# A second feed-forward block whose inner layer is multiplied as seven products of sums, with the inner features taken in two halves

## The chip, the core and the metric

The kernel runs on one core of one Trainium2 chip. The metric is the device time of that core in microseconds (us): 1461.32 us is the median of three runs (1461.11 to 1463.19). The engines of the core are called PE (TensorE, matrix products), DVE (VectorE), ACT (ScalarE), POOL (GpSimd) and SP (SyncE, which here issues most of the DMA transfers). PE writes its sums into PSUM, which has eight banks; a bank holds one result of 128 rows by up to 512 numbers in fp32.

## The reference, cut to what matters

Three stages follow one another: an attention with head mixing (batch 4, 12 heads, 448 positions), a gated feed-forward layer, and a second feed-forward layer. Attention gives 1792 tokens of 768 features. The feed-forward weights arrive as 64-bit floats.

```python
# x: 1792 x 768, from attention
gate = 1.0 / (1.0 + np.exp(-(x @ w_gate)))        # 768 -> 1536
x = (gate * (x @ w_val)) @ w_out                  # 1536 -> 768
h = x @ w2_in                                     # 768 -> 2048
out = (h * (1.0 / (1.0 + np.exp(-1.702 * h)))) @ w2_out   # 2048 -> 768
```

## The kernel before, in words

Attention comes first; its order is worked out by a planner and the change leaves it as it is. Then the class `Ffn` works through the 1792 tokens in two blocks of 896 (two batches of 448, called h = 0 and 1). Each block passes four stages, named after the PSUM tile in which PE sums: gate and value (`pg`, `pv`; in the second block `pq`), `py` (w_out), `ph` (w2_in) and `po` (w2_out).

Numbers are kept as two parts: a rounded high part (a copy or cast on ACT) and the rest (a subtraction on DVE, here called the low part). A product of two such numbers takes three matmuls: high by high, high by low, low by high. A weight piece is 128 x 384, that is three 128 x 128 tiles; one step of the pipeline takes one piece, its "unit". In the first block each piece is loaded as 64-bit floats, converted by one ACT pass and four DVE passes (`bits`, `conv1` to `conv4`), stored in DRAM (`kept`) and split into high and low (`high`, `low`, L732 and L737). In the second block the pieces come back from `kept`, two per load, and are only split. `take` and `ahead` issue these steps some units before PE needs them; five buffers of split weights (pool `w`) limit how far. What is put off with `after(n, f)` is issued n+1 units later, behind that unit's weight work.

In the second block, gate and value are already done as seven products of sums in place of eight (`quarters`): the activations are cut into four quarters (two token halves by two halves of the 768 features), the weights of two neighbouring feature tiles too, and seven combinations are multiplied, 14 units of 9 matmuls for a gate-and-value pair of tiles (`ORDER`: 1, 2, 6, 5, 7, 4, 3, each for q = 0 gate and q = 1 value). DVE forms the weight sums (`sum`, L707) and, in `finish` (L845), the sums of the products, ACT saves three running sums per q (`save`, L841). The activation sums for it are formed during `po` of the first block (`next_x`).

`ph` is made of 16 feature tiles, each two units of 18 matmuls (128 x 448), all eight quarter products. `gated` (L809 to L815) then takes, for one token half after the other, the sigmoid (ACT), the product with the sum in PSUM (DVE) and the two parts. `po` sums all 16 feature tiles in PSUM for two column halves n of 384: 16 units of 21 matmuls (seven token tiles by three), for which it holds four pairs of banks. At the end of each n the seven sums are copied out by DVE and ACT in turn (L1003) and stored (L1005).

PSUM is handed out in pairs of banks by `banks` (L802). Every engine works through its own instructions in the order in which they were issued, so the order of the code is the order of the work.

Of the kernel before, what the change touches and what calls it, by code (L numbers as in the profile page):

```python
# [518 lines left out]
class Ffn:  # L519
# [9 lines left out]

    KG = 3  # L530
# [7 lines left out]
    def __init__(self, ctx, tc, xd, kept, w_gate, w_val, w_out, w2_in, w2_out, out):  # L538
# [18 lines left out]
        for n in range(self.NN):  # L557
            self.pieces += [self.block(w2_out, k0, 1, n * self.PW, self.PW) for k0 in range(K2)]
        self.N0 = len(self.pieces)

        self.items = [(i, i + 1) for i in range(self.N0)]
        self.units = [None] * self.N0
        for j in range(0, K1, 2):
            at = len(self.units)
            n = len(self.items)
            for f in range(2):
                for g in range(2):
                    self.items.append((4 * (j + f) + 2 * g, at + (10 + g if f == 0 else 14 + g)))
            for p in self.ORDER:
                for g in range(2):  # L570
                    self.units.append((p, n + g, n + 2 + g))
        for i in range(o1, self.N0, 2):
            at = len(self.units)
            self.units += [(0, len(self.items), x) for x in range(2)]
            self.items.append((i, at + 3))
# [14 lines left out]
    def open(self):  # L590
# [4 lines left out]
        self.xy_p = pool("xy", 2 * self.KD + 1, **rt)  # L595
# [3 lines left out]
        p0 = pool("ps0", 2, space=PSUM, **rt)  # L599
        self.pools = [p0, p0]  # L600
        self.X = [[self.form() for _ in range(2)] for _ in range(self.KD)]

    def form(self):

        return self.xy_p.tile([128, 2, self.S], F32R, tag="xy", name="xy")
# [39 lines left out]
    def early(self, i):  # L645
        if len(self.going) <= i:
            acc = self.banks(("pg", "pv")[i])
# [11 lines left out]
    def stage(self):  # L659
        i = self.items[len(self.staged)][0]  # L660
        st = self.wst_p.tile([128, self.PW, 2], U32, tag="ws", name="ws")
        if len(self.staged) < self.N0:
# [7 lines left out]
    def bits(self, i):  # L670
        if i < self.N0:
            c = self.wc_p.tile([128, self.PW], U32, tag="wc", name="wc")
            self.nc.scalar.activation(c.bitcast(F32), self.staged[i][:, :, 1].bitcast(F32), AF.Abs)
            self.conv[i] = c

    def conv1(self, i):
        if i < self.N0:
# [4 lines left out]
    def conv2(self, i):  # L682
        if i < self.N0:
# [4 lines left out]
    def conv3(self, i):  # L688
        if i < self.N0:
            c = self.conv[i]  # L690
            self.nc.vector.scalar_tensor_tensor(out=c, in0=self.staged[i][:, :, 1], scalar=0xC0000000, in1=c,  # L691
                                                op0=ALU.bitwise_and, op1=ALU.bitwise_or)

    def conv4(self, i):
        if i < self.N0:
            c = self.conv[i]
            self.nc.vector.scalar_tensor_tensor(out=c, in0=self.staged[i][:, :, 0], scalar=29, in1=c,  # L697
                                                op0=ALU.logical_shift_right, op1=ALU.bitwise_or)
            self.nc.sync.dma_start(self.kept[i], c.bitcast(F32))

    def sum(self, i):

        if self.units[i] is None or self.units[i][0] == 0:
            return
        p, n0, n1 = self.units[i]
# [358 lines left out]
```

## Time and profile before

| what | value |
|---|---|
| median of three runs | 1461.32 us |
| the profiled execution's own time | 1458.4 us |
| its span in the trace | 1456.7 us |
| PE busy | 1425.2 us, 98% of the span, 9264 matmuls |
| DVE busy | 919.2 us, 63%, 2180 instructions |
| ACT busy | 732.2 us, 50%, 1694 instructions |
| `pq`, second block (974.2 to 1127.5 us) | PE never idle, DVE busy 114.67 of 153.3 us |

The table is read from the top: the span says how long the core worked, the busy times how much of it each engine had an instruction under way. Busy times count an instruction from its start to its acknowledged end, so two neighbouring ones overlap a little; how often an engine can start one is read from the starts in a list by time. Matmuls overlap in the same way: one lasts some 365 ns in the record and the next begins about 203 ns after it.

### The profile page before, as it was taken

How to read it: one execution, taken by the hardware profiler on the slowest of the kernel's cores; microseconds unless marked ns; L12 is line 12 of the kernel's file. 1: busy time of each engine (PE TensorE's matmuls, PEld its weight loads, DVE VectorE, ACT ScalarE, POOL GpSimd, SP SyncE). 2: the span in 40 equal slices, each digit the busy share in tenths (PEclk: the TensorE clock that was granted, in tenths of full speed). 3: DMA queues.
4: the chain of work that ended last, by engine and by line, in shares of the span. 5: the costliest groups of instructions: out<-in, count | busy, mean ns of one | idle time of the engine just before them, and what ended most of it. 6: DMA issues, size and time to landing. Idle time of an engine off the chain costs nothing.

```text
span 1456.7 us, 25413 instructions
## 1 busy us (share of the span) xinstructions
PE 1425.2 (98%) x9264; PEld 1304.6 (90%) x9264; DVE 919.2 (63%) x2180; ACT 732.2 (50%) x1694; POOL 189.3 (13%) x175
## 2 busy tenths in 40 slices
PE   7999999999998999999999989999999999999998
PEld 5878888888887999999999889999999999999998
DVE  6677787787777767676667887757877223444121
ACT  6877887887886444433245443335555112443110
POOL 3343443443444000000000000000000000000000
PEclk9999999999999999999999999999999999999999
DMA  6645435422444645465635466722222211111121
GB/s 172 176 136 152 138 125 150 141 109 97 139 157 145 209 147 177 148 177 166 188 114 156 151 228 192 269 76 67 64 66 76 66 52 47 54 55 56 54 71 38
DMA packets 180045, 182.26 MB, mean 125 GB/s; under 512 B 66364, under 2 KB 175824, under 8 KB 179920
## 3 DMA queue, kind: packets, MB, share of 16 engines
q1 hardware_dynamic: 178896, 180.40, 40.1%
q8 instruction: 73, 1.20, 0.3%
q14 instruction: 52, 0.43, 0.1%
q10 hardware_dynamic: 960, 0.23, 0.1%
q0 software_dynamic: 64, 0.01, 0.0%
HBM read 104.31 MB, written 37.75 MB: 98 GB/s over the span
## 4 chain that ended last, share of the span: by engine, by line
PE 79%; DVE 9%; ACT 6%; DMA 4%; issue 2%; SPq 0%; POOL 0%; DVEq 0%; ACTq 0%; POOLq 0%
PE po L998 16%; PE py L793 12%; PE pq L836 11%; PE ph L793 9%; PE pso L325 7%; PE pv L793 6%; PE pg L793 6%; PE psv L344 5%; PE psp L280 4%; PE psq L240 3%; DMA ws<-in_moe_w_in_dram 2%; ACT ex L294 1%; DMA gt<-sc 1%; DVE wc L691 1%; DVE st L287 1%
## 5 line engine op out<-in xcount | busy, mean ns | idle before, releaser
L998 PE MATMUL po<-w,hx 128*128 128x384 f32 x1344 | 239.9, 340 | 3.4 <-DVE sg L814 2.6
L998 PEld LDWEIGHTS po<-w,hx 128*128 128x128 f32 x1344 | 238.8, 189 | 4.3 <-DVE sg L814 2.9
L793 PE MATMUL ph<-xy,w 128*128 128x448 f32 x1152 | 236.1, 366 | 1.9 <-DVE w L737 1.9
L793 PEld LDWEIGHTS ph<-xy,w 128*128 128x128 f32 x1152 | 215.7, 188 | 22.0 <-DVE w L737 4.9
L273 POOL TENSOR_TENSOR ghl<-gt,ghl 120x448 fp32r<-120x448 f32 (+1 forms) x151 | 174.0, 1158 | 259.6 <-ACT ghl L209 184.5
L325 PEld LDWEIGHTS pso<-w,ex 120*112 120x112 f32 (+1 forms) x1440 | 159.6, 177 | 29.9 <-ACT w L307 10.2
L325 PE MATMUL pso<-w,ex 120*112 120x120 f32 (+1 forms) x1440 | 171.7, 270 | 11.4 <-DVE xo L363 3.8
L793 PE MATMUL py<-g,w 128*128 128x448 f32 x864 | 176.0, 366 | 0.0
L793 PEld LDWEIGHTS py<-g,w 128*128 128x128 f32 x864 | 162.3, 188 | 13.4
L732 ACT CAST w<-wc 128x384 fp32r<-128x384 f32 x136 | 69.8, 513 | 160.7 <-DVE wc L697 115.0
L737 DVE TENSOR_TENSOR w<-ws,w 128x384 fp32r<-128x384 f32 x124 | 68.6, 554 | 127.2 <-ACT w L732 127.2
L732 ACT CAST w<-ws 128x384 fp32r<-128x384 f32 x124 | 62.1, 513 | 170.3 <-PE po L998 85.4
L280 PE MATMUL psp<-ghl,wphl 120*120 120x448 f32 x540 | 137.5, 383 | 2.4 <-POOL ghl L273 1.5
L287 DVE TENSOR_REDUCE st<-psp 120x1 f32<-120x448 f32 x180 | 108.5, 614 | 41.2 <-PE psp L280 40.8
L294 ACT ACTIVATE ex<-psp,st 120x448 f32<-120x448 f32 x180 | 113.0, 631 | 11.7 <-DVE st L287 7.2
L280 PEld LDWEIGHTS psp<-ghl,wphl 120*120 120x120 f32 x540 | 89.1, 182 | 16.3 <-issue 3.9
L209 ACT CAST ghl<-gt 120x448 fp32r<-120x448 f32 (+1 forms) x139 | 77.8, 563 | 50.6 <-PE psp L280 44.2
L814 DVE TENSOR_TENSOR sg<-sg,ph 128x448 f32<-128x448 f32 x64 | 39.8, 622 | 96.3 <-ACT sg L813 96.3
L836 PE MATMUL pq<-xy,w 128*128 128x448 f32 x468 | 98.0, 365 | 0.0
L836 PEld LDWEIGHTS pq<-xy,w 128*128 128x128 f32 x468 | 87.9, 188 | 7.1
L793 PE MATMUL pg<-xy,w 128*128 128x448 f32 x432 | 91.2, 368 | 0.0
L793 PE MATMUL pv<-xy,w 128*128 128x448 f32 x432 | 89.5, 365 | 0.0
(86 smaller groups left out, 1950.2 us busy)
## 6 DMA issues: line engine op xcount, KB each, us to landing
gt<-sc SPq DMA_DIRECT2D x172, 210.0 KB
kept<-wc SPq DMA_DIRECT2D x136, 192.0 KB
ws<-kept SPq DMA_DIRECT2D x68, 384.0 KB
ws<-in_moe_w_out_dram SPq DMA_DIRECT2D x56, 384.0 KB
ws<-in_moe_w_in_dram SPq DMA_DIRECT2D x32, 384.0 KB
ws<-in_moe_w_gate_dram SPq DMA_DIRECT2D x24, 384.0 KB
ws<-in_moe_w_val_dram SPq DMA_DIRECT2D x24, 384.0 KB
nat<-in_k_dram SPq DMA_DIRECT2D x48, 112.0 KB
```

Of the source, the lines that this page charges most:

```text
L209: (eng.copy if eng is nc.scalar else eng.tensor_copy)(dst, src)
L273: eng.tensor_tensor(out=t[:m, 1], in0=gt.pop(s)[:m], in1=t[:m, 0].bitcast(F32), op=ALU.subtract)
L280: nc.tensor.matmul(ps[:m, :S], wphl[:m, wp, :m], t[:m, gp], start=(i == 0), stop=(i == 2))
L287: nc.vector.tensor_reduce(out=st[:m, 0:1], in_=pre[s][:m, :S], axis=AX.X, op=ALU.max, negate=True)
L294: nc.scalar.activation(t[:m], pre.pop(s)[:m, :S], AF.Exp, bias=st[:m, 0:1], scale=1.0, accum_out=st[:m, 1:2])
L325: nc.tensor.matmul(ps[:JC, c, :, :n], e[:m, c * JC:(c + 1) * JC], w[:m, :, :n], start=True, stop=True)
L344: nc.tensor.matmul(ps[a * 64:a * 64 + 64, r, :n], vt[b][:, g, c, :], a_t[:, c, g, :n], start=(c == 0), stop=(c == NJ - 1), tile_position=( ...
L732: self.nc.scalar.copy(w[:, 0], self.source(i))
L737: self.nc.vector.tensor_tensor(out=w[:, 1], in0=self.source(i), in1=w[:, 0].bitcast(F32), op=ALU.subtract)
L793: self.nc.tensor.matmul(acc[:, hb, :self.S], st, act[k0 + kc][hb][:, ap], start=(k0 + kc == 0 and part == 0 and ap == 0), stop=(k0 + kc == ...
L836: nc.tensor.matmul(x, st, A[p][c][:, ap], start=(first and c + part + ap == 0), stop=(c == self.KG - 1 and part == 1), skip_group_check=no ...
L998: nc.tensor.matmul(po[tk][:, :PW], HX[kc][:, part, tk * 128:(tk + 1) * 128], w[:, wp], start=(kc == 0 and part == 0 and wp == 0), stop=(kc ...
```

## The change

`ph` of the second block uses `quarters` too. `quarters` now takes a function `done` that says what becomes of a finished sum: `gates` is the old use, `inner` the new one (four feature tiles at a time; the sigmoid goes back into a PSUM bank and DVE multiplies by it from there). The activation sums are formed by `next_y` during `py` of the second block. The 2048 inner features are taken in two halves, in both blocks: eight tiles of `ph`, then `po` over these eight for both n, whose sums are kept in SBUF (`kept` tiles in pool `gh`); then the other eight, and `po` again, to which the kept sums are added. `banks` hands out single banks, `po` takes seven. `gated` issues both sigmoids, then both products, then both splits. `next_x` forms all of the second block's first activation sums in 12 units of the second `po` half. Pool `gh` has 12 buffers in place of 16; the 21 tiles of the sums have a pool of their own.

```diff
+    def inner(self, HX):
+        def done(q, f, h, y, bank):
+            self.after(0, lambda: self.nc.scalar.activation(bank, y, AF.Sigmoid, scale=1.702))
+            self.after(1, lambda: self.tt(y, y, bank, ALU.mult))
+            self.after(2, lambda: self.hilo(HX[2 * q + f][:, :, h * self.S:(h + 1) * self.S], y))
+        self.quarters(self.A, done)
...
     def gated(self, g, pg, pv, scale=1.0):
-        for h in range(2):
-            sg = self.temp("sg")
-            self.nc.scalar.activation(sg, pg[:, h, :self.S], AF.Sigmoid, scale=scale)
-            self.nc.vector.tensor_tensor(out=sg, in0=sg, in1=pv[:, h, :self.S], op=ALU.mult)
-            self.hilo(g[:, :, h], sg)
+        sg = [self.temp("sg") for _ in range(2)]
+        for h in range(2):
+            self.nc.scalar.activation(sg[h], pg[h][:, :self.S], AF.Sigmoid, scale=scale)
+        for h in range(2):
+            self.nc.vector.tensor_tensor(out=sg[h], in0=sg[h], in1=pv[h][:, :self.S], op=ALU.mult)
+        for h in range(2):
+            self.hilo(g[:, :, h], sg[h])
...
+    def next_y(self, m, py):
+        A, KG, S = self.A, self.KG, self.S
+        c = m % KG
+        x, y = (py[h][:, :S] for h in range(2))
+        if m < KG:
+            for p in (1, 7):
+                A[p].append(self.form())
+            t = self.ys[c] = [self.temp("ys") for _ in range(2)]
+            self.nc.scalar.copy(t[0], x)
+            self.nc.scalar.copy(t[1], y)
+            self.tt(x, t[0], t[1], ALU.subtract)
+            self.hilo(A[1][c], t[0])
+            self.hilo(A[7][c], x)
+        else:
+            for p in (2, 6, 5, 4, 3):
+                A[p].append(self.form())
+            t0, t1 = self.ys[c]
+            self.hilo(A[2][c], x)
+            self.tt(t1, t1, y, ALU.add)
+            self.tt(t0, t1, t0, ALU.subtract)
+            self.flush()
+            self.hilo(A[6][c], t0)
+            self.tt(x, x, t0, ALU.subtract)
+            self.hilo(A[5][c], t1)
+            self.hilo(A[4][c], y)
+            self.hilo(A[3][c], x)
...
-            for f in range(K2):
-                ph = self.banks("ph")
-                self.products(ph, Y)
...
+            for half in range(2):
+                HX = []
+                for f in range(0, HK, 4):
+                    for _ in range(4):
+                        HX.append(gh_p.tile([128, 2, 2 * S], F32R, tag="gh", name="hx"))
+                        if not t:
+                            ph = self.banks("ph", 2)
+                            self.products(ph, Y)
+                            self.gated(HX[-1].rearrange("p a (h s) -> p a h s", h=2), ph, ph, 1.702)
+                    if t:
+                        self.inner(HX[f:])
+                self.flush()
...
+                for n in range(self.NN):
+                    po = self.banks("po", NT)
+                    for kc in range(HK):
...
+                    self.flush()
                     for tk in range(NT):
+                        i = n * NT + tk
+                        if half == 0:
...
+                            (nc.scalar.copy if tk % 2 else nc.vector.tensor_copy)(kept[i], po[tk][:, :PW])
+                        else:
...
+                            if tk % 2:
+                                nc.scalar.copy(ot, po[tk][:, :PW])
+                                self.after(0, lambda ot=ot, i=i, out=out: (self.tt(ot, ot, kept[i], ALU.add),
+                                                                           nc.sync.dma_start(out, ot)))
+                            else:
+                                self.tt(ot, kept[i], po[tk][:, :PW], ALU.add)
+                                nc.sync.dma_start(out, ot)
+                    self.flush()
```

Three places show how the instructions move. The first is DVE in `ph` of the second block. Before, one feature tile (36 matmuls) is two low parts of weights (`w`), two products with the sum (`sg<-sg,ph`) and two low parts of results (`hx`):

```order
L819 TENSOR_TENSOR hx<-sg,hx 128x448 x2
L737 TENSOR_TENSOR w<-ws,w 128x384
L814 TENSOR_TENSOR sg<-sg,ph 128x448 x2
L737 TENSOR_TENSOR w<-ws,w 128x384
L819 TENSOR_TENSOR hx<-sg,hx 128x448 x2
```

Now a piece of the last six units of a group of four tiles, in the same stage (`wt` are sums of weights; `s<-s,pq` at L892 is `finish`, at L937 the product with the sigmoid):

```order
L892 TENSOR_TENSOR s<-s,pq 128x448
L937 TENSOR_TENSOR w<-ws,w 128x384
L743 TENSOR_TENSOR wt<-ws 128x384
L743 TENSOR_TENSOR wt<-ws,wt 128x384
L937 TENSOR_TENSOR c<-c,pq 128x448
L892 TENSOR_TENSOR s<-s,pq 128x448
L937 TENSOR_TENSOR w<-ws,w 128x384
L743 TENSOR_TENSOR wt<-ws 128x384
L743 TENSOR_TENSOR wt<-ws,wt 128x384
L937 TENSOR_TENSOR s<-s,pq 128x448
L864 TENSOR_TENSOR hx<-c,hx 128x448
L892 TENSOR_TENSOR s<-s,pq 128x448
```

What was 24 DVE instructions for four tiles is now 46, for 126 matmuls in place of 144.

The second place is ACT in `ph` of the first block, one feature tile with the two weight pieces behind it (`wc` and `w` are the passes on weights). Before:

```order
L813 ACTIVATE sg<-ph 128x448
L818 CAST hx<-sg 128x448
L813 ACTIVATE sg<-ph 128x448
L818 CAST hx<-sg 128x448
L673 ACTIVATE wc<-ws 128x384
L732 CAST w<-wc 128x384
```

Now:

```order
L768 CAST w<-wc 128x384
L856 ACTIVATE sg<-ph 128x448 x2
L863 CAST hx<-sg 128x448 x2
L709 ACTIVATE wc<-ws 128x384
L768 CAST w<-wc 128x384
```

The second sigmoid stands ahead of the first cast, which has to wait for DVE's product.

The third place is the end of the program on DVE, from the last parts of `ph` on. Before:

```order
L737 TENSOR_TENSOR w<-ws,w 128x384
L819 TENSOR_TENSOR hx<-sg,hx 128x448 x2
L737 TENSOR_TENSOR w<-ws,w 128x384 x15
L1003 COPY ot<-po 128x384 x4
L737 TENSOR_TENSOR w<-ws,w 128x384 x13
L1003 COPY ot<-po 128x384 x4
```

Now:

```order
L864 TENSOR_TENSOR hx<-s,hx 128x448 x3
L937 TENSOR_TENSOR w<-ws,w 128x384 x7
L937 TENSOR_TENSOR ot<-kept,po 128x384 x4
L937 TENSOR_TENSOR ot<-ot,kept 128x384 x3
L937 TENSOR_TENSOR w<-ws,w 128x384 x6
L937 TENSOR_TENSOR ot<-kept,po 128x384 x4
L937 TENSOR_TENSOR ot<-ot,kept 128x384 x3
```

The three additions for the sums that ACT copies stand behind DVE's own four.

## Rows read from the trace of the kernel before

**Rows 1.** The page: busy time of each engine, share of the span, instructions.
```profile
PE 1425.2 (98%) x9264; PEld 1304.6 (90%) x9264; DVE 919.2 (63%) x2180; ACT 732.2 (50%) x1694; POOL 189.3 (13%) x175
```

**Rows 2.** PE by time: start, length, line, tiles, count, idle time before and releaser.
```profile
642.64 86.58 PE L793 MATMUL py<-g,w 128*128 128x448 f32 x432
729.06 66.97 PE L793 MATMUL ph<-xy,w 128*128 128x448 f32 x328
796.29 7.56 PE L793 MATMUL ph<-xy,w 128*128 128x448 f32 x36 [0.26 <-DVE w L737]
...
850.00 0.34 PE L998 MATMUL po<-w,hx 128*128 128x384 f32 x1
851.12 3.27 PE L998 MATMUL po<-w,hx 128*128 128x384 f32 x17 [0.78 <-DVE w L737]
857.01 117.34 PE L998 MATMUL po<-w,hx 128*128 128x384 f32 x654 [2.62 <-DVE sg L814]
974.19 11.11 PE L836 MATMUL pq<-xy,w 128*128 128x448 f32 x54
...
996.30 14.76 PE L836 MATMUL pq<-xy,w 128*128 128x448 f32 x72
...
1021.81 14.76 PE L836 MATMUL pq<-xy,w 128*128 128x448 f32 x72
...
1127.52 89.44 PE L793 MATMUL py<-g,w 128*128 128x448 f32 x432
1216.80 116.91 PE L793 MATMUL ph<-xy,w 128*128 128x448 f32 x576
1333.55 118.95 PE L998 MATMUL po<-w,hx 128*128 128x384 f32 x672
```

**Rows 3.** Stretches: length, busy time of PE, PEld, DVE, ACT, POOL, PEclk, DMA.
```profile
857.00:861.00 4.00, 3.99 (x14) 3.99 (x15) 4.00 (x11) 2.01 (x4) 0.00 (x0) 0.57 0.36 98
...
974.20:1127.50 153.30, 153.30 (x757) 141.98 (x757) 114.67 (x223) 83.11 (x168) 0.00 (x0) 1.00 0.23 71
```

**Rows 4.** DVE by time in `ph` of the first block.
```profile
828.55 0.35 DVE L679 TENSOR_SCALAR wc<-wc 128x384 f32<-128x384 f32 x1
...
830.02 0.56 DVE L737 TENSOR_TENSOR w<-wc,w 128x384 fp32r<-128x384 f32 x1
831.13 0.62 DVE L814 TENSOR_TENSOR sg<-sg,ph 128x448 f32<-128x448 f32 x1 [0.56 <-ACT sg L813]
832.83 0.62 DVE L814 TENSOR_TENSOR sg<-sg,ph 128x448 f32<-128x448 f32 x1 [1.08 <-ACT sg L813]
```

**Rows 5.** DVE by time in `pq` of the second block.
```profile
994.35 0.62 DVE L851 TENSOR_TENSOR c<-c 128x448 f32<-128x448 f32 x1
994.88 0.61 DVE L845 TENSOR_TENSOR s<-s,pq 128x448 f32<-128x448 f32 x1
995.41 0.55 DVE L737 TENSOR_TENSOR w<-ws,w 128x384 fp32r<-128x384 f32 x1
995.88 0.55 DVE L707 TENSOR_TENSOR wt<-ws 128x384 f32<-128x384 f32 x1
```

**Rows 6.** ACT by line in `pq` (974.2 to 1127.5): busy, mean ns, idle before.
```profile
L732 ACT CAST w<-wt 128x384 fp32r<-128x384 f32 x48 | 24.6, 513 | 14.7 <-PE pq L836 9.3 <-ACT w L732 5.5
L841 ACT COPY s<-pq 128x448 f32<-128x448 f32 x36 | 19.2, 535 | 20.7 <-PE pq L836 19.7 <-ACT w L732 0.9
...
L848 ACT ACTIVATE s<-s 128x448 f32<-128x448 f32 x18 | 10.4, 578 | 0.6
L818 ACT CAST g<-s 128x448 fp32r<-128x448 f32 x17 | 9.7, 568 | 8.3 <-DVE s L851 8.3
```

**Rows 7.** The end by time, PE, DVE and SP's queue.
```profile
1445.81 6.70 PE L998 MATMUL po<-w,hx 128*128 128x384 f32 x37
...
1450.48 3.46 SPq L1005 DMA_DIRECT2D out_dram<-ot  x7
...
1452.01 1.09 DVE L1003 COPY ot<-po 128x384 f32<-128x384 f32 x2 [0.51 <-PE po L998]
```

More of the change, by code (lines that the diff above doesn't have):

```diff
@@ L556, in __init__, with whole, kept_pair, kept_sums @@
             self.pieces += [self.block(w2_in, k0, KG, f * 128, 128) for k0 in range(0, KD, KG)]
[L557 to L564, printed above, removed]
+        o2 = len(self.pieces) - 2 * K2
+        o3 = len(self.pieces)
+        HK = K2 // 2
+        for half in range(2):
+            for n in range(self.NN):
+                self.pieces += [self.block(w2_out, k0, 1, n * self.PW, self.PW) for k0 in range(half * HK, half * HK + HK)]
+        self.items = []
+        self.units = []
+        def whole(i):
+            self.units.append(("f", len(self.items), i))
+            self.items.append(("f", i, len(self.units)))
+        def kept_pair(i):
+            u = len(self.units)
+            self.units += [("p", len(self.items), x) for x in range(2)]
+            self.items.append(("k", i, u + 3))
+        def kept_sums(i):
+            u = len(self.units)
             n = len(self.items)
@@ L758, in ahead, with flush @@
     def ahead(self):
-        while self.step < min(self.taken + (4 if self.taken < self.N0 else 5), len(self.units) + 2):
+        n = 5 if self.units[self.taken - 1][0] == "s" else 4
+        while self.step < min(self.taken + n, len(self.units) + 2):
             self.split()
-        now, self.later = [f for n, f in self.later if n <= 0], [(n - 1, f) for n, f in self.later if n > 0]
-        for f in now:
-            f()
+        self.flush(False)
+    def flush(self, whole=True):
+        while self.later:
+            now, self.later = [f for n, f in self.later if n <= 0], [(n - 1, f) for n, f in self.later if n > 0]
+            for f in now:
+                f()
+            if not whole:
+                break
     def after(self, n, f):
@@ L800, in products, with banks @@
             pass
-    def banks(self, name):
-        self.turn += 1
-        return self.pools[(self.turn - 1) % len(self.pools)].tile([128, 2, 512], F32, tag="ps", name=name)
+    def banks(self, name, n):
+        self.turn += n
+        return [self.pools[i % len(self.pools)].tile([128, 512], F32, tag="ps", name=name)
+                for i in range(self.turn - n, self.turn)]
     def temp(self, name):
@@ L989, in run @@
[L989 to L1005 removed]
+                if t:
+                    self.next_y(m, py)
+                else:
+                    Y.append([self.form() for _ in range(2)])
+                    for h in range(2):
+                        self.hilo(Y[m][h], py[h][:, :S])
```

306 lines of the change are left out of this document (150 added, 156 removed).

## The prediction

> **What bounds the kernel now.** I read the page's engine line first, then PE by time over the second half, then the stretches by stage, then DVE and ACT inside the stages that change. PE is busy 1425.2 of 1456.7 us [rows 1]: what counts is how many matmuls there are and where PE waits. In PE by time the reader is to see two things. The second block's `ph` runs without a gap, 1333.55 - 1216.80 = 116.75 us for 576 matmuls, 202.7 ns each [rows 2]. The first block's `ph` does the same 576 from 729.06 to 850.00, 120.94 us: after nine of sixteen tiles (328 matmuls) PE begins to wait at each tile for DVE's low part of the weights, 0.26 us in the row shown. Then at the start of `po` it waits 0.78 and 2.62 us [rows 2]. Behind these waits the clock falls: granted 0.57 from 857 to 861, and full again later [rows 3]. `pq`, which works as the new stage will, has PE busy in all of its 153.3 us, DVE in 75% of it [rows 3].
>
> **The change part by part.**
>
> *Matmuls.* `ph` of the second block is 576 matmuls; seven of eight products make it 4 groups of 14 units of 9, that is 504. `po` keeps its 1344. So 72 go. A group of 126 took 1021.81 - 996.30 = 25.51 us in `pq` [rows 2], 202.5 ns each, the same as in `ph`. 72 x 0.2027 = **14.6 us saved**, if PE is fed as well as in `pq`.
>
> *Can DVE feed it?* DVE starts: from 994.35 to 994.88 and on to 995.41 an instruction of 448 columns takes 0.53 us, whether it reads SBUF alone or PSUM; one of 384 takes 0.47 [rows 5]. A group of `inner` has 46: 8 sums of `finish`, 8 products with the sigmoid and 8 low parts of results (24 x 0.53 = 12.7), 14 low parts and 8 sums of weights (22 x 0.47 = 10.3), together 23.1 us against 25.5 us of PE. `pq` has 38 (four products and four low parts of results fewer): 18.8. It is not even over the group. I stepped the issued order against unit ends 1.82 us apart: after units 8 to 13, which each end in a sum, DVE is up to some 2.5 us late; before, and in the three units that follow, it catches up. The low part of a weight stands in the order behind the sum of unit i and is needed by unit i+4, three units or 5.5 us later. So the lateness does not reach PE, with some 3 us to spare. ACT has 14 casts, 6 saves, 8 sigmoids and 8 casts of results: 14 x 0.513 + 6 x 0.535 + 8 x 0.578 + 8 x 0.568 = 19.6 us at most [rows 6], covered. The sigmoid that writes into PSUM has no row; by the nearest rows it lies between the save's 535 and the sigmoid's 578 ns [rows 6], 0.4 us per group on an engine with 6 us left, so nothing either way. I take zero for all this; if the cover is gone, each us that a group of DVE takes beyond 25.5 us is 4 us in all, less the 5.5 us of lead at the start of each half.
>
> The rows just read show no difference between an SBUF and a PSUM operand on DVE. The Trainium skill says otherwise: Perfetto Trace Analysis, Optimizing Scalar/DVE Operations, gives DVE about 60 ns of access overhead on SBUF and about 125 on PSUM. By that, the 16 instructions per group that read PSUM would cost 16 x 0.065 = 1.0 us more (an estimate from that page), 24.1 of 25.5 us; the sum would stay as it is, but rival B would be likelier, about one in five. By the rows it is one in eight, and I hold to the rows.
>
> *Waits of the first block.* In `ph` DVE works in a cycle of 7.84 us: ACT alternates sigmoid, cast, sigmoid, cast, and DVE waits 0.56 and then 1.08 us for the two sigmoids [rows 4]. Its own work is two weight pieces (four passes from 828.55 to 830.02 and 0.47 for the low part, 1.94 each) and four instructions of 0.53, 6.0 us; PE's tile is 36 x 0.2027 = 7.3 us. With both sigmoids ahead of the casts the 1.08 goes, and DVE is faster than PE. Besides, after eight tiles comes `po` for 16 units of 3.72 us, with 1.94 us of weights each: time to get ahead, and before, the first eight tiles had no wait. So the 120.94 - 116.75 = 4.2 us go. `po` of the first block took 974.19 - 850.00 = 124.19, of the second 1452.5 - 1333.55 = 118.95 [rows 2]; the 5.2 us between them are the two waits and the fallen clock. `po` took all eight banks and waited for the last pair's products; now it takes seven single ones, and the two banks of the last tile come to it as the seventh and not at all. I count **9.4 us saved**, from 0 (the waits turn up elsewhere) to 9.4.
>
> What takes their place? The new ends of `po` copy out seven sums while PE is at the last unit, bank by bank, and an eighth bank is free for the next: as at the middle of `po` today, where no wait is listed. Tightest is the second half of the first block, where 33 DVE instructions of `next_x` (17.5 us) now fall into 12 units instead of 32: steps 2 to 11 hold 20 x 0.97 + 17.5 + 3.3 for seven additions, 40.2 us, against ten units of 37.2. By the lookahead of `ahead` DVE is some two units (7 us) ahead there, so the 3 us are eaten from the lead. I take 0, with 0 to 3 us.
>
> *Sums in two steps.* 14 copies in each block: DVE 8 x 0.47, ACT 6, behind PE's last unit of a `po`; and additions in place of copies. Hidden, except at the end of the program: there DVE's three additions for ACT's sums stand behind its own four. Before, the last copy ended at 1453.1 and SP issued until 1453.94 [rows 7]; three times 0.47 put the last issue **1.4 us later**. Bounds 0 (the issues were the slower: seven in 3.46 us) and 2.5 (three transfers behind one another).
>
> *`next_y`.* During `py` of the second block, three or eight DVE instructions per 14.9 us step; nothing. After the last step the first units need their weights: three DVE instructions and one low part (2.1 us) stand ahead of the low part for unit 2, needed 3.7 us after the end of `py`. Close, covered.
>
> *Other placement.* Tiles get other addresses. That a stage's pace can differ is seen in `py`: the same 432 matmuls from 642.64 to 729.06 and from 1127.52 to 1216.80 [rows 2], 86.4 and 89.3 us, with no wait listed. I give the new 102 us of `inner` 3% of it either way, 3 us, and expect none.
>
> The sum against the profiled execution: 1458.4 - 14.6 - 9.4 + 1.4 = 1435.8 us. The median of the runs is 2.9 us above that execution, so **1438.7, say 1439 us**; its own range is 1434 to 1444.
>
> **The rivals.**
>
> *B, DVE bounds the new stage.* For: 23.1 of 25.5 us leaves little, and the first block's `ph` shows how waits for ACT make DVE the bound at less work, 1.64 us idle per two results [rows 4]. Against: there the sigmoid was issued just before the product that needs it, here two units ahead, and `pq` shows no wait. If each of the eight results of a group idled DVE by 0.82 us, a group takes 29.7 us, 4.2 us more, 16.7 in all: 1456. With half of that, 1447.
>
> *C, the first block's waits stay or move.* Then only 14.6 - 1.4 are won: 1448. For: DVE has 53% of its time in weights there, and there are now two starts of `po`. Against: the two sigmoids in a row, and the rest after eight tiles.
>
> *D, slower: the ring of seven temporaries.* A group of `inner` takes eight buffers of pool `s` (six saves, two `c`). The second save of a group gets the buffer that the sixth result of the group before gives back, which by my stepping DVE reads last some 3.4 us after ACT could begin. ACT works in order, so casts of weights behind it wait too. If DVE is later than I think, PE stops once in each of four groups: with 5 us each, and 4 us at the 0.57 of [rows 3] behind it (1.7 us lost), 27 us: 1466. It decides against the change from 5.6 us per group on, that is when DVE is 11 us late at the end of a group (5.5 of lead and 5.6). Against: I find 2.5.
> For that fall of the clock the Trainium skill has a rule too: TensorE: Matmul & The Clock Gate, A second HAM failure mode, tells of kernels whose groups cycle through PSUM banks and lose the clock in small gaps. The trace does not bear it out here: `pq`, in groups of 9 and with a bank for each sum, ran at 1.00 throughout [rows 3].
>
> That the change does not do what it says is excluded for the count: the order has 126 matmuls a group.
>
> **How the numbers follow.** The forecast has 0.70, B 0.12, C 0.08, D 0.07; 0.03 is for a loss of all that is won, about no change. The range goes from 1434 to 1452, which leaves out D, the upper half of B and the last: about 0.15. A measurement of this kernel tells a change from none at about 0.2%, 3 us. Faster: forecast, B and C, 0.90; same 0.03; slower 0.07.
>
> **What would show it.** Right: `ph` of the first block in two pieces of 58.4 us without a listed wait; `inner` in four groups of 25.5 us with PE busy throughout at clock 1.00 and DVE near 100% busy by the record; every `po` at 177 ns a matmul; the end 1.4 us longer. Wrong: PE in `inner` waiting for `w` from DVE (B) or ACT waiting for a low part of `hx` ahead of a save and PE behind it (D); a wait at the start of a `po` or in the last units of the first block (C); or the pace of a stage off by several per cent without a wait.

## The result and the profile after

The changed kernel ran in 1448.38 us (median of four runs, 1440.88 to 1452.13) against 1462.26 us before (four runs): a ratio of 0.9896, 95% interval 0.9848 to 0.9943. Timed twice more, later, it took 1446.7 us (ratio 0.9878, 0.984 to 0.9916) and 1442.03 us (0.9855, 0.9832 to 0.9877). It is faster by 1.0 to 1.5%, the range of 1434 to 1452 holds it, and the point, 1439, was too low by 9.4 us in the first comparison (7.7 and 3.0 in the later ones).

The page of the profiled execution (1452.13 us, span 1450.4) answers to [rows 1] with 72 matmuls fewer, and with 134 DVE instructions more:

```profile
PE 1416.9 (98%) x9192; PEld 1293.6 (89%) x9192; DVE 984.9 (68%) x2314; ACT 767.3 (53%) x1769; POOL 189.4 (13%) x175
```

PE by time in the changed kernel, with the columns of [rows 2]; the new inner stage appears under the tile `pq`, in two pieces of 252 matmuls:

```profile
652.08 89.44 PE L835 MATMUL py<-g,w 128*128 128x448 f32 x432
741.36 58.66 PE L835 MATMUL ph<-xy,w 128*128 128x448 f32 x288
799.86 59.52 PE L1076 MATMUL po<-w,hx 128*128 128x384 f32 x336
859.22 58.55 PE L835 MATMUL ph<-xy,w 128*128 128x448 f32 x288
917.61 30.36 PE L1076 MATMUL po<-w,hx 128*128 128x384 f32 x171
949.69 0.79 PE L1076 MATMUL po<-w,hx 128*128 128x384 f32 x3 [1.72 <-ACT ot L1091]
952.15 30.41 PE L1076 MATMUL po<-w,hx 128*128 128x384 f32 x162 [1.68 <-DVE ot L937]
982.40 153.72 PE L883 MATMUL pq<-xy,w 128*128 128x448 f32 x756
1135.96 86.58 PE L835 MATMUL py<-g,w 128*128 128x448 f32 x432
1222.37 51.89 PE L883 MATMUL pq<-xy,w 128*128 128x448 f32 x252
1274.10 59.52 PE L1076 MATMUL po<-w,hx 128*128 128x384 f32 x336
1333.46 51.97 PE L883 MATMUL pq<-xy,w 128*128 128x448 f32 x252
1385.27 59.89 PE L1076 MATMUL po<-w,hx 128*128 128x384 f32 x336
```

The reader is to see three things. No wait is listed from 982 us to the end. The waits of the first block's `ph` and of the start of its `po` [rows 2] are gone. In their place PE waits twice in the middle of the second `po`, 1.72 and 1.68 us, where the seven sums of the first column half are taken out.

The lengths of the stages come from such rows, each from its start to the next one's (us). Beside the two first profiles stand a second one of the changed kernel, and two of experiments that are told below:

| | before | after | after, again | old kernel, two sigmoids ahead | early third (the repeat) |
|---|---|---|---|---|---|
| start of `py`, first block | 642.64 | 652.08 | 644.36 | 643.46 | 644.68 |
| `py` | 86.42 | 89.28 | 86.39 | 86.42 | 86.42 |
| `ph` | 120.94 | 116.89 | 116.77 | 116.74 | 116.76 |
| `po` | 124.19 | 124.15 | 124.29 | 118.71 | 118.72 |
| `pq`, second block | 153.33 | 153.56 | 153.56 | 153.33 | 155.11 |
| `py` | 89.28 | 86.41 | 86.42 | 89.28 | 89.28 |
| `ph` or `inner` | 116.75 | 103.54 | 103.53 | 116.75 | 103.62 |
| `po` | 118.95 | 119.25 | 119.24 | 118.88 | 119.23 |
| PE's last matmul to the end | 4.2 | 5.2 | 5.2 | 4.2 | 4.2 |
| span | 1456.7 | 1450.4 | 1439.8 | 1447.8 | 1438.0 |

From before to after the stages that the change touches give -13.2 (`inner`), -4.05 (`ph`), 0.0 (`po` of the first block), +0.3 (`po` of the second), +0.2 (`pq`) and +1.0 (the end), together -15.8. The spans differ by 6.3 us only, because `py` of the first block starts 9.4 us later (the two `py` swap their lengths, which cancels). 6.2 of the 9.4 stand in attention, ahead of the first `pv` matmul (481.0 us for 474.8), and 3.2 in the first gate-and-value stage behind it (171.1 for 167.8). The change reaches that stage too, by `gated` and the single banks, but the second profile of the same kernel takes 167.9 us there, as the kernel before does. That profile starts `py` 7.7 us sooner and is 10.6 us shorter; its other stages are the same but for `py`.

The stretches, with the columns of [rows 3]: the first piece of `inner`, and the waits.

```profile
1222.40:1274.10 51.70, 51.70 (x253) 47.25 (x252) 45.46 (x89) 35.95 (x74) 0.00 (x0) 1.00 0.23 68
949.00:960.00 11.00, 8.63 (x39) 8.32 (x40) 11.00 (x26) 3.89 (x9) 0.00 (x0) 0.84 0.72 228
```

PE is busy in all of this piece at clock 1.00 (so it is in the second), and DVE in 88% of it (45.46 of 51.7 us). Behind the two waits the granted clock is 0.84 on the mean of 11 us: 0.69 from 952 to 955 and 0.74 from 955 to 958, 1.00 on either side. So part of these 6 us passes at the lower of its two levels, 1.2 GHz.

What DVE does before those waits, by time, and ACT's first copies:

```profile
925.88 0.55 DVE L937 TENSOR_TENSOR w<-wc,w 128x384 fp32r<-128x384 f32 x1
929.30 0.62 DVE L937 TENSOR_TENSOR xs<-xy,xs 128x448 f32<-128x448 f32 x1 [2.87 <-DMA xs<-xd]
...
949.17 0.84 ACT L1091 COPY ot<-po 128x384 f32<-128x384 f32 x2
...
951.54 1.95 DVE L937 TENSOR_TENSOR ot<-kept,po 128x384 f32<-128x384 f32 x4
```

And the queue of SP, which issues the loads that it waits for:

```profile
922.10 0.33 SPq L735 DMA_DIRECT2D kept<-wc  x1
...
923.00 2.36 SPq L811 DMA_DIRECT2D xy<-xd  x3
925.42 0.43 SPq L964 DMA_DIRECT2D xs<-xd  x1
```

SP issues the first loads of `next_x` from 923.00 to 925.85. Before that it stood from 917.35 to 922.10 in front of the store of a converted weight, which waits for a pass of DVE that ends at 922.07: DVE's own weight work holds up the load that DVE then waits for. DVE reaches the sum that needs the load at 926.4 and stands for 2.87 us. The weights and sums that follow leave no gap up to 951.54, when DVE takes the first of its four sums out of PSUM. ACT, which has casts of `next_x` to do as well, takes its first at 949.17. PE has ended the seven sums at 947.3 (917.61 + 168 matmuls of 0.177) and has one free bank to go on with. Its first wait ends with ACT's copy, its second with DVE's. That is where the lead went.

ACT and DVE by line in the first piece of `inner` (busy, mean ns, idle before; `s<-s,pq` at L937 is the product with the sigmoid):

```profile
L930 ACT ACTIVATE pq<-s 128x448 f32<-128x448 f32 x11 | 6.0, 548 | 4.2 <-DVE s L892 4.2
...
L937 DVE TENSOR_TENSOR s<-s,pq 128x448 f32<-128x448 f32 x10 | 6.1, 613 | 0.0
L864 DVE TENSOR_TENSOR hx<-s,hx 128x448 fp32r<-128x448 f32 x8 | 4.9, 616 | 0.0
L892 DVE TENSOR_TENSOR c<-s,pq 128x448 f32<-128x448 f32 x4 | 2.5, 620 | 5.1 <-ACT s L888 5.1
```

The sigmoid that writes into PSUM takes 548 ns, between the two rows that bounded it. DVE's product that reads PSUM takes 613 ns and the low part that does not 616.

The end by time, which answers to [rows 7]:

```profile
1445.19 0.55 DVE L937 TENSOR_TENSOR ot<-kept,po 128x384 f32<-128x384 f32 x1 [0.51 <-PE po L1076]
1445.67 1.49 DVE L937 TENSOR_TENSOR ot<-ot,kept 128x384 f32<-128x384 f32 x3
1446.24 1.32 SPq L1093 DMA_DIRECT2D out_dram<-ot  x3
```

DVE adds the three sums that ACT copied behind its own four; SP issues their stores last.

### The profile page after: what moved, and what is told of

Same layout as the page of the kernel before. It is cut to its first block, busy times and chain, and to the rows that moved or that the text cites. A ratio compares the mean times of both kernels' runs of the same rounds, so it can differ in the third digit from the quotient of the medians.

```text
span 1450.4 us, 25506 instructions
## 1 busy us (share of the span) xinstructions
PE 1416.9 (98%) x9192; PEld 1293.6 (89%) x9192; DVE 984.9 (68%) x2314; ACT 767.3 (53%) x1769; POOL 189.4 (13%) x175
## 4 chain that ended last, share of the span: by engine, by line
PE 84%; DVE 6%; ACT 5%; DMA 2%; issue 2%; SPq 0%; POOL 0%; DVEq 0%; ACTq 0%; POOLq 0%
PE pq L883 17%; PE po L1076 14%; PE py L835 12%; PE ph L835 8%; PE pso L326 7%; PE pv L835 6%; PE pg L835 6%; PE psv L345 5%; PE psp L281 4%; PE psq L241 3%; ACT ex L295 2%; DMA gt<-sc 2%; ACT ghl L210 1%; DVE st L288 1%; ACT w L308 1%
## 5 line engine op out<-in xcount | busy, mean ns | idle before, releaser
L883 PE MATMUL pq<-xy,w 128*128 128x448 f32 x1260 | 257.6, 366 | 0.0
L883 PEld LDWEIGHTS pq<-xy,w 128*128 128x128 f32 x1260 | 236.5, 188 | 20.5
L768 ACT CAST w<-ws 128x384 fp32r<-128x384 f32 x116 | 58.7, 515 | 115.0 <-PE po L1076 63.1
L835 PE MATMUL ph<-xy,w 128*128 128x448 f32 x576 | 117.2, 365 | 0.0
L835 PEld LDWEIGHTS ph<-xy,w 128*128 128x128 f32 x576 | 108.1, 188 | 8.7
L937 DVE TENSOR_TENSOR w<-ws,w 128x384 fp32r<-128x384 f32 x116 | 62.7, 553 | 47.6 <-ACT w L768 47.6
L835 PEld LDWEIGHTS pg<-xy,w 128*128 128x128 f32 x432 | 81.6, 189 | 8.2
```

What stands on the lines that cost most here:

```text
L768: self.nc.scalar.copy(w[:, 0], self.source(i))
L835: self.nc.tensor.matmul(acc[hb][:, :self.S], st, act[k0 + kc][hb][:, ap], start=(k0 + kc == 0 and part == 0 and ap == 0), stop=(k0 + kc == ...
L883: nc.tensor.matmul(x, st, A[p][c][:, ap], start=(first and c + part + ap == 0), stop=(c == self.KG - 1 and part == 1), skip_group_check=no ...
L937: self.nc.vector.tensor_tensor(out=dst, in0=x, in1=y, op=op)
```

## The experiments

Line numbers in rows are those of each kernel. "One execution" means a single, profiled one and its time beside runs of the kernel before.

**Both kernels again.** No edit.

> The kernel before, unchanged, profiled a second time, to learn what one execution tells. Theory 1 (the pace of a stage is a state of the execution): the 432 matmuls of py take 200.0 or 206.7 ns each in either block, not the same as in the first profile (200.0 in the first block, 206.7 in the second); attention's end moves by some us. Theory 2 (the pace belongs to the program): 200.0 and 206.7 again in the same places, and the stages within 0.3 us of the first profile.

> The changed kernel, unchanged, profiled a second time. Theory 1 (state of the execution): the first block's gate-and-value stage and py need not be at 206.7 ns again, and py may start up to 9 us earlier than the 652.1 us of the first profile. Theory 2 (the program): the same paces and the same 652 us. Both: the waits of 1.7 and 1.7 us in the second po half of the first block are there again, since they come from the order of the work, and PE has none in ph and in the seven-product stages.

One execution each: 1464.95 us for the kernel before, 1441.52 for the changed one (median of 13 runs of the kernel before, beside them: 1465.72). The kernel before, by time from `py` of the second block:

```profile
1131.75 89.44 PE L793 MATMUL py<-g,w 128*128 128x448 f32 x432
1221.03 119.19 PE L793 MATMUL ph<-xy,w 128*128 128x448 f32 x576
1340.06 118.95 PE L998 MATMUL po<-w,hx 128*128 128x384 f32 x672
```

The same `ph` that took 116.75 us takes 119.03 here (1340.06 - 1221.03), 206.7 ns a matmul for 202.7, with no wait. So a stage has more than one pace for the same program, and one pair of profiles does not tell a change of 3 us in a stage from this. (`py` has 86.41 and 89.28 us in the same places as in the first profile, as the second theory said; `ph`, and `pq` with 155.99 us for 153.33, have not.) The changed kernel shows its two waits again (1.86 and 1.68 us): these belong to the program. The late start of `py` does not.

**`next_x` spread over 15 units in place of 12.** First step at the same place. A pair (c, i) is third c of `next_x`, part i: loads, sums, low parts.

```diff
-        for c, i in {0: [(0, 0)], 2: [(0, 1)], 3: [(0, 2), (1, 0)], 5: [(1, 1)], 6: [(1, 2)], 8: [(2, 0)],
-                     10: [(2, 1)], 11: [(2, 2)]}.get(step, []):
+        for c, i in {0: [(0, 0)], 3: [(0, 1)], 4: [(0, 2)], 8: [(1, 0)], 10: [(1, 1)], 11: [(1, 2), (2, 0)],
+                     13: [(2, 1)], 14: [(2, 2)]}.get(step, []):
```

> The changed kernel with one table altered: when next_x forms the second block's activation sums. The first third loads at unit 0 and is used at units 3 and 4 (before: 2 and 3), the two others wait until the mid-stage copies are done (units 8 to 14). Theory (DVE waits for a load of x, loses its lead, and the copies of the mid-stage come 6 us late): both 1.7 us waits go, the clock does not fall there, and that second po half takes 59.4 in place of 64.8 us, 5.4 us off the median. Rival (the copies are late because single banks leave PE only one spare bank): the waits stay, no change within 1 us.

1440.63 us (four runs; ratio to before 0.9819, 0.9777 to 0.9861). The one execution of the changed kernel beside it took 1441.52, so the 5.4 us are not settled by the times. PE by time:

```profile
906.53 59.52 PE L1076 MATMUL po<-w,hx 128*128 128x384 f32 x336
965.89 4.27 PE L883 MATMUL pq<-xy,w 128*128 128x448 f32 x20
971.61 149.80 PE L883 MATMUL pq<-xy,w 128*128 128x448 f32 x736 [1.45 <-DVE w L937]
```

Both waits are gone and `po` takes 59.36 us in place of 64.9. DVE still waits for the loads of x, 0.85 us, and is in time. So it is the place of `next_x` that made PE wait, and not the single banks by themselves. Which part of it, this run does not tell, because the edit does two things: the first third's sums stand one unit further behind their load, and the second third (11 DVE instructions, some 5.8 us) moves behind the copies. By the rows of the changed kernel both count: without its 2.87 us DVE would have taken its first sum at 948.7, still 1.4 us after PE's end (an estimate from these rows). A part comes back as 1.45 us at the start of `pq`: the last steps, units 13 and 14, now stand too near to it. Net 5.5 - 1.8 = some 3.7 us (`pq` 155.36).

**The two halves alone:** the second block's `ph` with all eight products, in halves as in the first block; the rest of the change stays, but for `next_y` and the weight sums, which only the seven products need.

```diff
...
-                        if not t:
-                            ph = self.banks("ph", 2)
-                            self.products(ph, Y)
-                            self.gated(HX[-1].rearrange("p a (h s) -> p a h s", h=2), ph, ph, 1.702)
-                    if t:
-                        self.inner(HX[f:])
+                        ph = self.banks("ph", 2)
+                        self.products(ph, Y)
+                        self.gated(HX[-1].rearrange("p a (h s) -> p a h s", h=2), ph, ph, 1.702)
```

> The changed kernel without the seven products in w2_in: both blocks multiply w2_in in full (576 matmuls each), but in halves, with w2_out in two steps, single banks and both sigmoids ahead. Theory (prediction: 14.6 us come from the 72 matmuls, the rest from the waits of the first block): second block's ph 2 x 58.4 us, 14.6 us slower than the changed kernel and some 3 to 5 us faster than before; the same 1.7 and 1.7 us waits in the first block. Rival (the halves and single banks gain or lose much themselves): more than 4 us off that.

1463.04 us (ten runs) against 1465.72 (ratio 0.9971, 0.995 to 0.9992). The second block, by time:

```profile
1217.85 58.40 PE L835 MATMUL ph<-xy,w 128*128 128x448 f32 x288
1276.09 59.52 PE L1070 MATMUL po<-w,hx 128*128 128x384 f32 x336
1335.44 58.42 PE L835 MATMUL ph<-xy,w 128*128 128x448 f32 x288
1393.70 59.51 PE L1070 MATMUL po<-w,hx 128*128 128x384 f32 x336
```

`ph` takes 58.24 us in the first half (1276.09 - 1217.85) and 58.26 in the second (1393.70 - 1335.44), 58.24 + 58.26 = 116.5 us where `inner` takes 103.5: the seven products are worth 13.0 us. All else in the change is worth 2.7 us at the median, which the stages that it touches give too: -4.05 in `ph` of the first block, -0.2 in its `po` (waits of 1.55 and 1.67 us are here as well) and +1.6 at the end. (This profile's span is 1459.0 us all the same: its `py` starts at 647.73, 5.1 us later than in the first profile of the kernel before.)

**Old order in `gated`,** the rest of the change as it is: sigmoid, product, split for one token half, then for the other.

```diff
-        for h in range(2):
-            self.nc.scalar.activation(sg[h], pg[h][:, :self.S], AF.Sigmoid, scale=scale)
-        for h in range(2):
-            self.nc.vector.tensor_tensor(out=sg[h], in0=sg[h], in1=pv[h][:, :self.S], op=ALU.mult)
-        for h in range(2):
-            self.hilo(g[:, :, h], sg[h])
+        for h in range(2):
+            sg = self.temp("sg")
+            self.nc.scalar.activation(sg, pg[h][:, :self.S], AF.Sigmoid, scale=scale)
+            self.nc.vector.tensor_tensor(out=sg, in0=sg, in1=pv[h][:, :self.S], op=ALU.mult)
+            self.hilo(g[:, :, h], sg)
```

> The changed kernel with the old order in gated: sigmoid, product, cast of one token half, then of the other. Theory A (the break after eight tiles alone is enough): both ph halves of the first block take 58.4 us without a wait, at most 1 us at the start of po. Theory B (it is the two sigmoids in a row that took the waits away): PE waits 0.3 us per tile again from some tile on and 0.8 and 2.6 us at the start of po, with the clock falling behind them, up to 9 us in all.

One execution, 1457.38 us. PE by time in the first block:

```profile
791.47 0.34 PE L1074 MATMUL po<-w,hx 128*128 128x384 f32 x1
792.26 3.26 PE L1074 MATMUL po<-w,hx 128*128 128x384 f32 x17 [0.45 <-DVE w L935]
796.46 4.68 PE L1074 MATMUL po<-w,hx 128*128 128x384 f32 x25 [0.94 <-DVE sg L857]
...
950.18 1.33 PE L1074 MATMUL po<-w,hx 128*128 128x384 f32 x3 [3.08 <-ACT ot L1089]
```

`ph` has no wait listed in either half: a break after eight tiles is enough for that. The starts of `po` wait all the same, and with DVE late from there the second `po` takes 71.5 us (911.72 to 983.21). The waits at its starts are shorter than in the kernel before (0.45 + 0.94 + 0.23 us for 0.78 + 2.62), so single banks and the break help there too; but it is the order of the sigmoids that frees the starts of `po`, as the next experiment shows.

**The kernel before with the new order in `gated` alone.** The same lines put into the old kernel, on its pairs of banks.

```diff
+        sg = [self.temp("sg") for _ in range(2)]
         for h in range(2):
-            sg = self.temp("sg")
-            self.nc.scalar.activation(sg, pg[:, h, :self.S], AF.Sigmoid, scale=scale)
-            self.nc.vector.tensor_tensor(out=sg, in0=sg, in1=pv[:, h, :self.S], op=ALU.mult)
-            self.hilo(g[:, :, h], sg)
+            self.nc.scalar.activation(sg[h], pg[:, h, :self.S], AF.Sigmoid, scale=scale)
+        for h in range(2):
+            self.nc.vector.tensor_tensor(out=sg[h], in0=sg[h], in1=pv[:, h, :self.S], op=ALU.mult)
+        for h in range(2):
+            self.hilo(g[:, :, h], sg[h])
```

> The kernel before with one part of the change alone: gated issues both sigmoids, then both products, then both splits. Theory (the cycle of 7.84 us per tile was DVE waiting 1.64 us for two sigmoids; without the second wait DVE needs under 7.3): ph of the first block takes 116.9 us in place of 120.9, without waits in its later tiles; at the start of po the waits of 0.8 and 2.6 us shrink to at most 1.5 in all, and the clock does not fall there: 4 to 9 us gained in the trace from the first ph to the first seven-product stage. Rival (only the break after eight tiles helps): ph stays at 120.7 to 120.9 us.

One execution, 1449.48 us against 1463.81 (span 1447.8, against 1456.7 in the first profile of the kernel before). PE by time, first block:

```profile
729.88 116.90 PE L793 MATMUL ph<-xy,w 128*128 128x448 f32 x576
846.62 118.88 PE L1000 MATMUL po<-w,hx 128*128 128x384 f32 x672
965.33 11.11 PE L838 MATMUL pq<-xy,w 128*128 128x448 f32 x54
```

And DVE, with what it still waits for:

```profile
818.63 1.15 DVE L815 TENSOR_TENSOR sg<-sg,ph 128x448 f32<-128x448 f32 x2 [1.19 <-ACT sg L813]
```

No wait is left in either stage: 116.74 and 118.71 us, against 120.94 and 124.19. The order inside `gated` is worth 4.2 + 5.5 = 9.7 us, without halves and without single banks. DVE now waits once per feature tile, 1.19 us, in place of 0.56 and 1.08 [rows 4], and that is slack.

**The early third:** `next_x` over both halves of the first block's inner features, 28 units, and in the last `po` the additions for ACT's sums issued at once.

```diff
-        for c, i in {0: [(0, 0)], 2: [(0, 1)], 3: [(0, 2), (1, 0)], 5: [(1, 1)], 6: [(1, 2)], 8: [(2, 0)],
-                     10: [(2, 1)], 11: [(2, 2)]}.get(step, []):
+        for c, i in {9: [(0, 0)], 12: [(0, 1)], 13: [(0, 2)], 16: [(1, 0)], 19: [(1, 1)], 20: [(1, 2)], 24: [(2, 0)],
+                     26: [(2, 1)], 27: [(2, 2)]}.get(step, []):
...
-                if half:
+                if half and t:
...
-                        if half and t + 1 < self.NBLK:
-                            self.next_x(n * HK + kc)
+                        if t + 1 < self.NBLK:
+                            self.next_x((half * self.NN + n) * HK + kc)
...
-                                self.after(0, lambda ot=ot, i=i, out=out: (self.tt(ot, ot, kept[i], ALU.add),
-                                                                           nc.sync.dma_start(out, ot)))
+                                self.tt(ot, ot, kept[i], ALU.add)
+                                nc.sync.dma_start(out, ot)
```

> The changed kernel with the first third of next_x moved into the first w2_out half of the first block (where DVE has only weights to do), the other two thirds before and behind the mid-stage copies of the second half, and the three additions at the end of the program issued in line instead of behind the four. Theory (the lost lead costs 5.4 us, and e1 gave 1.8 of it back because its last third came too late for the first gate unit; the additions behind cost 1.0): no wait of PE from the first ph to the end, second po half 59.4 us, the seven-product stage starts without the 1.5 us wait, the end 4.2 us after PE's last matmul instead of 5.2; median 6 us below the changed kernel's. Rival (the loads of x, not their place, are what DVE waits for): a new wait in the first half, gain under 3 us.

> The changed kernel, unchanged, beside the version with the early third and the kernel before on the same chip. Every theory: the two 1.7 us waits in the first block; median 14 to 22 us below the kernel before, since the paces of the stages differ from execution to execution by some us each.

> The version with the early third and the additions in line, timed once more beside the changed kernel. Theory: no wait from the first ph to the end again, 4 to 7 us below the changed kernel's median. Rival (its lead was the paces of a few executions): within 2 us of it.

> The changed kernel once more, beside the version with the early third: 16 to 20 us below the kernel before, 4 to 7 us above the version with the early third.

The first time 1441.81 us (ratio 0.9838, 0.9804 to 0.9872) beside 1446.7 for the changed kernel; the second time 1441.59 (0.9845, 0.9826 to 0.9864) beside 1442.03. The two profiles of the second time have the same paces, so their rows can be laid side by side. The changed kernel:

```profile
909.60 30.36 PE L1076 MATMUL po<-w,hx 128*128 128x384 f32 x171
941.51 0.79 PE L1076 MATMUL po<-w,hx 128*128 128x384 f32 x3 [1.55 <-ACT ot L1091]
943.97 28.88 PE L1076 MATMUL po<-w,hx 128*128 128x384 f32 x162 [1.67 <-DVE ot L937]
972.69 155.28 PE L883 MATMUL pq<-xy,w 128*128 128x448 f32 x756
```

The early third:

```profile
907.22 59.52 PE L1076 MATMUL po<-w,hx 128*128 128x384 f32 x336
966.58 155.28 PE L883 MATMUL pq<-xy,w 128*128 128x448 f32 x756
```

`po` takes 59.36 us for 63.09, and the end is 1.1 us shorter: 4.8 us from `py` to the end. In the changed kernel's profile the waits are there and the clock stays up (the row after them is 28.88 us long, not 30.41), so 3.7 of the 5.4 us come with the waits themselves and the rest only where the clock falls. The medians differ by 4.9 us the first time, where 6 was expected, and by 0.4 the second, where 4 to 7 was expected and the rival said within 2 (the changed kernel came out 21.8 us below the kernel before, for 16 to 20 expected): the gain is plain in the trace and not settled by the times. Nor do the times tell this version from `next_x` over 15 units (1440.63 us, ratio 0.9819). No wait of PE is listed from the first `ph` to the end, `pq` starts without one, and the last steps stand at unit 11 again: that bears out that units 13 and 14 were too late.

**DVE with 8 and with 16 instructions more per group** of `inner`: one or two maxima of a result with itself, 448 columns, written into a bank that is done with (the diff shows the kernel with one).

```diff
             self.after(1, lambda: self.tt(y, y, bank, ALU.mult))
+            for _ in range(1):
+                self.after(1, lambda: self.tt(bank, y, y, ALU.max))
```

> The changed kernel with 8 more DVE instructions of 448 columns per group of inner, 4.2 us, half of the earlier experiment. By DVE's 23.1 us per group it needs 27.3 where PE needs 25.5: 1.8 us too much per group, 7 us over the four. Theory, as the experiment with 16 more corrected it (what DVE is late comes back as waits, in inner or at the start of the po behind it): waits of PE of 4 to 8 us in all, most of them at the starts of po, plus what the clock costs behind them. Rival (DVE had no room at all): 17 us of waits.

> The changed kernel with 16 more DVE instructions of 448 columns per group of inner (two behind each product with the sigmoid, their result is not used): 16 x 0.53 = 8.5 us. Theory (DVE needs 23.1 us per group and hides up to 25.5): 31.6 us per group, 6.1 us more on PE in each of four groups, less up to some 3 us of slack per half: inner takes 116 to 122 us in both halves together in place of 103.5. Rival B (DVE is at its limit already because of waits for ACT): all of the 8.5 us shows, 137 us.

One execution each: 1458.72 and 1488.78 us. With 8 more, PE by time at the start of the `po` behind the first piece (the piece itself has one wait, 0.33 us, <-DVE w):

```profile
1265.46 2.81 PE L1078 MATMUL po<-w,hx 128*128 128x384 f32 x15
1270.03 0.80 PE L1078 MATMUL po<-w,hx 128*128 128x384 f32 x3 [1.76 <-DVE pq L939]
1272.29 58.82 PE L1078 MATMUL po<-w,hx 128*128 128x384 f32 x318 [1.46 <-DVE pq L939]
```

The same start as a stretch, with the columns of [rows 3]:

```profile
1266.00:1280.00 14.00, 10.78 (x46) 10.13 (x46) 11.03 (x22) 5.28 (x11) 0.00 (x0) 0.76 0.26 82
```

With 16 more, the waits of PE over the execution (us in total, times, longest):

```profile
PE po L1078 <- DVE pq L939: 15.0, 6, 7.3
PE pq L883 <- DVE w L939: 10.2, 12, 1.8
```

By the prediction's rows a group with 8 more is 23.1 + 8 x 0.53 = 27.3 us of DVE, 1.8 over PE's 25.5; with 16 more 31.6, 6.1 over. Times four groups that is 7.2 and 24.4 us; the listed waits are 8.8 (0.33 + 1.76 + 1.46, and 0.33 + 4.55 + 0.40 in the second half; 4 to 8 was expected) and 25.2. By these sums hardly any of the lateness is forgiven. The agreement is looser than it looks: in the rows an extra instruction starts 0.65 us behind the product whose result it reads (1265.97 and 1266.62) and takes DVE 0.66 us, not 0.53, by which the two sums are some 11.5 and 33 us (an estimate from these rows). Either way 5.5 us of lead per half, 11 us in all, would have left next to no wait with 8 more, and 8.8 us are there: the lead did not pay for what is too much per group. With 8 more the lateness passes through `inner` almost unseen and is paid at the start of `po`, which waits for the last banks; with 16 more 10.2 us of the waits are in `inner` (117.9 us in both pieces, as expected) and 15.0 in `po`. Part of the cover at that place is used up without any extra: in the changed kernel DVE's last product of the first piece ends at 1276.97, 2.9 us after `po` began; with 8 more, 7.8 us after. One thing is not parted from DVE's time here: the waits end with the extra instruction (`pq` at L939), which writes into the bank and so holds it 0.7 us longer than the product alone would, or 1.3 with two.

With 8 more, the block from `inner` to PE's last matmul is 16.9 us longer than in the changed kernel (239.7 for 222.8 us). 8.8 of that are waits, 5.4 more lie in the two `po`, where the clock is at 0.76 in the 14 us around the waits, and 2.7 in `inner`, at clock 1.00. With 16 more it is 35.2 us longer. A loss near the rival's size comes out both times (17 and 34), but with 8 more half of it is not waiting for DVE.

## Why the prediction was right, and where it was not

*Matmuls, 14.6 us: right, 13.2 measured,* 13.0 against the same kernel with eight products. The 1.4 us between are pace: 103.54 us for 504 matmuls are 205.4 ns each in place of 202.7, within the 3 us kept for it. It is 103.53 to 103.62 us in all eight profiles that have this stage unaltered, so this pace is not that of one execution; why it is slower than `pq` at its fast pace (202.8 ns) stays open. The rows of `inner` show no wait.

*DVE can feed it: right.* It is busy in 88% of the first piece and 81% of the second (the prediction's sign was near 100%), waits itself (5.1 us of idle before `c<-s,pq`), and PE does not. Rival B fell, and D with it: no wait of PE for ACT is listed in `inner`. The waits of the two further kernels, and DVE's 45.46 us in a piece of two groups, lie near the 23.1 us per group. The claim that the 5.5 us of lead pay for what a group takes beyond 25.5 fell, though it cost nothing here, because a group of the changed kernel stays below that. The Trainium skill's figure for DVE reading PSUM (Perfetto Trace Analysis, Optimizing Scalar/DVE Operations) is not borne out by the new rows either: 613 ns with PSUM, 616 without.

*First block's `ph`, 4.2 us: right, 4.05.* The prediction named both the order of the sigmoids and the break after eight tiles. Either alone is enough.

*First block's `po`, 5.2 us: the step that failed, 0.0 measured.* The old waits did go, by the order of the sigmoids; single banks, which the prediction names for it, were not needed. The new ones came where the prediction looked, "33 DVE instructions of `next_x` (17.5 us) now fall into 12 units", and it gave them "0, with 0 to 3 us". They cost 5.4. Its sum of 40.2 us of DVE against 37.2 of PE ran over steps 2 to 11 and was made against a lead of two units, 7 us. But the banks are wanted at the end of unit 7: by then stand 22 of the 33 instructions and five weight pieces, without a gap from 929.30 to 951.54, and the additions of the first column half behind all of it. The first step also waits for loads that SP issues a moment before, 2.87 us, and PE had one free bank, that is three matmuls, to go on with. Behind the 3.4 us of waits the clock falls in three of the four profiles of this kernel. This is rival C in part: of the 9.4 us from waits, 4.05 were won. With `next_x` wider apart the whole 9.4 are there (`ph` and `po` 116.76 + 59.36 + 59.36 us, for 245.13 before), less 1.8 at the start of `pq`; with the early third they are there without that loss.

*The end, 1.4 us: right, 1.0,* and taken back by issuing the additions at once.

*`next_y` and the start of `inner`, nothing: right;* no wait at 1222.37.

*What is left.* By stages the change is worth 15.8 us, not 22.6. The first comparison shows 13.9, the later ones 17.6 and 21.8. At least a part of that spread is not the change's: the first profile lost 9.4 us ahead of `py`, the next one 1.7. What moves attention by so much in one execution and not in another stays open. The first `pv` stands at 474.8 to 476.4 us in the three profiles with the old kernel's pairs of banks and at 475.6 to 481.0 in the eleven with the change or a variant of it, so a loss of an us or two in attention through the change is not excluded. The times alone would not have shown which term failed: 1448.38 us is also the price of rival C, 1448, and that the last comparison comes near to the point is no success of the 5.2 us.

## What to carry to other kernels

Where a slack engine's work is pressed into a shorter stretch, count what it waits for at the front of that stretch and what stands queued behind it at the end, and not just its sum against the bound engine's. An engine's lead over PE was no budget here: lateness that `inner` hid was paid at the next change of stage, where the banks are wanted. And a small reordering that comes with a large change deserves a kernel of its own: two sigmoids ahead of two products gave 9.7 us alone by the stages of one profile, three quarters of what the 72 matmuls gave.

## What the runs showed that was not expected

The prediction read two lengths of `py` and put them down to where tiles lie. But one and the same stage of one and the same kernel differs in pace from execution to execution: 432 matmuls of `py` take 86.4 or 89.3 us (200.0 or 206.7 ns each), 576 of `ph` 116.75 or 119.03, 756 of `pq` 153.3, 155.1 or 156.0, at a granted clock of 1.00 and without a listed wait. In both profiles of the kernel before, the first `py` was the fast one; in the first profile of the changed kernel the second; in its repeat both. It is worth up to 3 us a stage, as much as some terms of the sum.
